# Scores of the first six head pairs: 32-bit matmuls of 64 rows, two side by side, in place of 128 rows half zeros, and a new table of schedule constants

## The chip, the cores and the metric

One core of a Trainium2 chip runs the whole program. The metric is the device time of one execution in microseconds (us); kernels are compared by the median of several executions. One further execution is recorded by the profiler, and all rows below come from it.

## The reference: what is computed

Attention with a threshold, then two feed-forward layers, all in 32-bit floats:

```
q, k, v: (4 batches, 8 heads, 576 positions, 64); tau = 0.02
scores = q @ k^T / sqrt(64)
keep a score if score >= rowmax - tau, else -1e9
attn   = exp(scores - rowmax) / (sum + 1e-9);  x = attn @ v      -> (2304 tokens, 512)
h = x @ w_in   (512 x 2048);  g = relu(h)^2;           x2  = g @ w_out
h = x2 @ w_in2 (512 x 2048);  g = max(0.01 h, h);      out = g @ w_out2
```

## The kernel before

**Attention** is cut into 16 units, one for each batch and pair of heads, and each unit into nine steps: four tiles of 128 query rows of the first head, four of the second, and one step for the last 64 rows of both heads (the tail). That makes 144 steps. In a step the scores of the tile against all 576 keys go into two PSUM banks of 288 columns (tile `s`, L585); VectorE takes the negated row maximum (`nb`, L595), ScalarE the exponential (`e`, L596), VectorE masks it by the threshold `th` and sums it (L602), and small operations give the reciprocal `r` (L605, L608).

For the first six pairs (`nat`, 54 steps) the score matmul runs on plain 32-bit floats. The tile `KH` holds the keys of both heads one above the other, 64 partitions each (head dimension 64), and `Q` holds the queries of a head in its own 64 partitions with zeros in the other 64 (L484). So each matmul contracts over 128 rows, half of them zeros: two matmuls of 128 x 288 for a step (one for each bank), four of 64 x 288 for a tail, where the two heads go to the lower and the upper half of the array's columns. Each 32-bit matmul stands as two records in the trace. From the seventh pair on, scores are products of rounded parts (`KH`, `KL`), and nothing of that is changed.

For the first four pairs (`nav`, 36 steps) the weights `e` are scaled, turned by TensorE (`pt`, L627, L628; five 128 x 128 transposes for a step), copied out (`PT`) and multiplied with the values in 32 bits (`o`, L688: five matmuls with 64 columns, that alternate between the lower and the upper half of the columns, the fifth with 64 rows only). Later pairs split the weights into two 16-bit parts (`P`) that DMA transposes.

**The first feed-forward layer** begins about step 41, in blocks of 256 tokens (`h` L736, `y` L762), on the first 12 of 16 blocks of the hidden dimension, and fills TensorE beside attention. Its weights `w0` to `w11` are unpacked and split on VectorE, ScalarE and GpSimd during the first 60 steps (L372 to L392). After attention the rest of the layer runs in blocks of 512 (L1166, L1208), and the second layer (L1055, L1133).

**The order** is made by a planner when the program is built. Each operation has a priority (its step plus a constant), a cost, and the engines that can do it; `order()` (L118) walks through modelled time, gives each free engine the most urgent ready operation, and weighs engines by the table `price`. The constants in `CFG` (L26) shift priorities, choose which steps split the weights in which way (`lb`), and how many hidden blocks run beside attention (`nf`). The engines then execute in that order, held only by semaphores. A score operation is entered here as two operations of cost 0.486, one for each bank; zeroing `Q` is an operation of its own that VectorE or GpSimd may do. SyncE issues nearly all DMAs; in the first unit the queries of head 0 are issued from ScalarE.

Of the kernel before, what the change touches and what calls it, by code (L numbers as in the profile page):

```python
# [18 lines left out]
P = 128  # L19
# [4 lines left out]
NFA = 12  # L24

CFG = dict(  # L26
    price=[{'V': 3.864, 'A': 2.379, 'G': 2.083},
           {'V': 2.058, 'A': 0.5, 'G': 0.597},
           {'V': 1.454, 'A': 0.877, 'G': 1.005},
           {'V': 4.321, 'A': 0.378, 'G': 0.428},  # L30
           {'V': 1.956, 'A': 0.969, 'G': 2.867},
           {'V': 3.46, 'A': 0.884, 'G': 4.561},
           {'V': 3.025, 'A': 1.381, 'G': 2.849}],
    lead1=0.344, xsg0=[0, 1], lbm=8, lb=[[0, 3, 5, 6], [1, 5], [0, 4], [2, 7]], xsm=4, xsg=[1, 2], dq=0.417, xu=False, pqk=-3.957,
    pd1=1.458, pex=1.266, pd2=1.468, ph=3.893, pl=-2.254, hu=True, bg=6.244, lead=4.309, w0=25.544, wstep=1.408, fend=1.015, tol=-0.227,
    hor=-0.102, xlead=5.334, nb=3, eb=4, pb=3, ptb=3, kvb=3, nat=[0, 1, 2, 3, 4, 5], nav=4, two=False, vb=2, tmb=1, gb=2, xb=1,
    w2step=-3.901, nf=[12, 12, 12, 12], wo=2.009, wold=[9, 10, 16], yal=40.578, xl2=26.294, xp=5, sp=2.609, ws=-16.879, ww=20.813, zc=3.74,
    th=0.397, x2l=2.921, sg0=1.043, sgstep=1.158, zb=1.416, zin=1.434, zout=1.386, slack=0.02, slackd=0.985, wrb=3, r1b=1, xrb=1,
)


# [223 lines left out]
def mmr(n):  # L265
    return (n + 32) / 2400.0


def move(nbytes):
    return nbytes / 220e3  # L270
# [7 lines left out]
def tile_kernel(ctx: ExitStack, tc: tile.TileContext, qT, kT, vv, w1, w2, tau, eye, out):  # L278
    nc = tc.nc
    B, H, D, S = qT.shape  # L280
# [4 lines left out]
    S2 = S // 2  # L285
    MAIN = S // P
    REM = S - MAIN * P
    NH = (S + P - 1) // P
    QB = S + REM
# [4 lines left out]
    f32 = lambda ap: ap.bitcast(F32)  # L294
# [12 lines left out]
    op = plan.op  # L307
# [29 lines left out]
    def dma(o, i, r, w, prio, nbytes, q=nc.sync, **k):  # L337
        return op(("S", 0.06, lambda: q.dma_start(out=o(), in_=i())), r, w, prio, dma=move(nbytes), **k)
# [116 lines left out]
    head, tail = [(0, 0), (0, 1), (1, 0), (1, 1)], [(0, 2), (0, 3), (None, MAIN), (1, 2), (1, 3)]  # L455
# [9 lines left out]
    def prep(n):  # L465
        b, p, what = order[n]
        o = pairs[n] = Box()
        o.b, o.nav, o.own, o.q = b, n < CFG["nav"], n >= NAV, [None] * 2
        h0 = 2 * p
        Q = val("att", "Q2", 2, [P, 2 * S + REM], F32 if n in CFG["nat"] else F32R)  # L470

        o.Q, o.pad = Q, []
        o.qs = qs = lambda h: Q.get()[:, h * QB:h * QB + S]
        at = lambda k: begin[n - 1] - 1.5 + CFG["bg"] + k * len(order[n - 1][2]) / 14 if n else -3.0 + k * 0.1
        raw = lambda: val("stage", "wraw", CFG["wrb"], [P, 2 * S], F32)
        if n in CFG["nat"]:

            kh = val("att", "KH", CFG["kvb"], [P, S], F32R)
            o.KH, o.KL = [kh] * 2, None
            for h in range(2):  # L480

                c0, c1 = (0, S) if len(what) > 5 else (0, 2 * P) if what is head and h == 0 else (REM, REM + 2 * P) if what is head else (2 * P, S) if h == 0 else (0, S)
                z = lambda h=h, c0=c0, c1=c1: qs(h)[(1 - h) * D:(2 - h) * D, c0:c1]
                zero = [("V", 0.55, lambda z=z: nc.vector.memset(z(), 0.0)), ("G", 0.57, lambda z=z: nc.gpsimd.memset(z(), 0.0))]  # L484
                if n:
                    op(zero, [], [Q], at(-1))
                else:
                    zq = Val()
                    o.pad = o.pad + [zq]
                    op(zero[1], [], [zq], at(-1))  # L490
                o.q[h] = c0, c1
            for h in range(2):
                c0, c1 = o.q[h]
                dma(lambda h=h, c0=c0, c1=c1: qs(h)[h * D:(h + 1) * D, c0:c1], lambda h=h, c0=c0, c1=c1: qT[b, h0 + h][:, c0:c1], [], [Q], at(0), D * (c1 - c0) * 4, q=nc.sync if n or h else nc.scalar, urgent=n == 0, issue=0.5 if n or h else 0.06)
            dma(lambda: f32(kh.get()), lambda: kT[b, h0:h0 + 2].rearrange("h d s -> (h d) s"), [], [kh], at(0) if n else -3.1, 2 * D * S * 4, urgent=n == 0)
            op(times(lambda: f32(kh.get()), S)[0:None if n else 1], [kh], [kh], at(1))
        else:
            qr, kr = raw(), raw()
            q3, k3 = (lambda: qr.get().rearrange("p (h s) -> p h s", h=2)), (lambda: kr.get().rearrange("p (h s) -> p h s", h=2))
            for j in range(2):  # L500
                dma(lambda j=j: q3()[j * D:(j + 1) * D], lambda: qT[b, h0:h0 + 2].rearrange("h d s -> d h s"), [], [qr], at(0), 2 * D * S * 4)
            for j in range(2):
                dma(lambda j=j: k3()[j * D:(j + 1) * D], lambda: kT[b, h0:h0 + 2].rearrange("h d s -> d h s"), [], [kr], at(1), 2 * D * S * 4)
            op([("G", 0.145, lambda: nc.gpsimd.memset(f32(Q.get()[:, S:QB]), 0.0))], [], [Q], at(0))
            op(times(kr.get, 2 * S), [kr], [kr], at(2))
            for h in range(2):
                op(rnd(lambda h=h: qs(h), lambda h=h: q3()[:, h], S, engs="AVG"), [qr], [Q], at(2))
            for h in range(2):
                op(sub(lambda h=h: qs(h)[D:P], lambda h=h: q3()[D:P, h], lambda h=h: f32(qs(h)[D:P]), S), [qr, Q], [Q], at(3 + h))
            o.KH, o.KL = [None] * 2, [None] * 2  # L510
            for h in range(2):
                kh = o.KH[h] = val("att", "KH", CFG["kvb"], [P, S], F32R)
                kl = o.KL[h] = val("att", "KL", CFG["kvb"], [P, S], F32R)
                op(rnd(lambda kh=kh: kh.get(), lambda h=h: k3()[:, h], S), [kr], [kh], at(5 + 2 * h))
                op(sub(lambda kl=kl: kl.get(), lambda h=h: k3()[:, h], lambda kh=kh: f32(kh.get()), S), [kr, kh], [kl], at(6 + 2 * h))


        va = o.VA = val("att", "VA", CFG["vb"], [P, NH, 2, D], F32)
        for h in range(2):
            dma(lambda h=h: va.get()[:, 0:MAIN, h], lambda h=h: vv[b, h0 + h, 0:MAIN * P].rearrange("(j p) d -> p j d", p=P), [], [va], at(9), 2 * MAIN * P * D * 4)  # L520
        for rows in (slice(0, REM), slice(P - REM, P)):
            dma(lambda rows=rows: va.get()[rows, MAIN], lambda: vv[b, h0:h0 + 2, MAIN * P:S].rearrange("h p d -> p h d"), [], [va], at(9), 4 * REM * D * 4)
        o.at = at
# [39 lines left out]
    def step(i):  # L563
        n, h, t = steps[i]
        o = pairs[n]
        s = Box()

        ps = val("ps_s", "s", 2, [P, 2, 512], F32)

        g_ = lambda g: slice(g * S2, (g + 1) * S2)  # L570
        if h is not None:
            q0 = h * (QB + REM) + t * P
            lhs = [(h, slice(0, P), slice(q0, q0 + P))]
        elif o.KL:
            lhs = [(0, slice(0, P), slice(MAIN * P, MAIN * P + P)), (1, slice(0, P), slice(S, S + P))]
        else:
            lhs = [(0, slice(0, REM), slice(MAIN * P, S)), (1, slice(REM, P), slice(QB, QB + REM))]

        def qk(g):
            if o.KL:  # L580
                ops = [(r, q, kk[hh]) for hh, r, q in lhs for kk in (o.KH, o.KL)]
            else:
                ops = [(r, q, o.KH[hh]) for hh, r, q in lhs]
            for k, (r, q, kk) in enumerate(ops):
                nc.tensor.matmul(ps.get()[r, g, 0:S2], lhsT=o.Q.get()[:, q], rhs=(kk.get() if o.KL else f32(kk.get()))[:, g_(g)],  # L585
                                 start=k == 0 or not o.KL, stop=k == len(ops) - 1 or not o.KL)
        heads = [hh for hh, _, _ in lhs]
        ks = [o.KH[0]] if o.KL is None else [k for hh in heads for k in (o.KH[hh], o.KL[hh])]
        for g in range(2):
            op(("T", 0.486 if o.KL is None and h is not None else 0.58 if o.KL is None else 2 * len(lhs) * mmr(S2), lambda g=g: qk(g)), [o.Q] + o.pad + ks, [ps], i + CFG["pqk"], True)  # L590
        pv = lambda: ps.get()[:, :, 0:S2]

        nb, th = (val("small", r, 4, [P, 1], F32) for r in ("nb", "th"))
# [4 lines left out]
        k = i % 2  # L598
# [556 lines left out]
    G = {}  # L1155
# [83 lines left out]
    z = [jobs[k * NU + NU - 1][0] + CFG["zb"] + k * CFG["zc"] for k in range(2)]  # L1239
# [20 lines left out]
    for s in range(n2 + 2):  # L1260
        pr = T0 + 2 * s
        work(s)
        if s < n2:
            layer, j, f = items[s]
# [5 lines left out]
        else:  # L1270
            k = s - n2
# [4 lines left out]
    t = n2 + 1.0  # L1276
# [75 lines left out]
```

## Time and profile before

| | |
|---|---|
| median of 3 runs | 1023.25 us (1022.06 to 1023.26) |
| profiled execution | 1027.67 us, of it 1025.9 us from the first to the last instruction |
| TensorE matmul busy | 977.7 us (95%) |
| VectorE | 841.9 us (82%) |
| ScalarE | 707.7 us (69%) |
| GpSimd | 374.9 us (37%) |

Busy time is the time in which an engine had at least one instruction under way; matmuls are pipelined, so a busy TensorE can still do more. The last scores run at 466 us, and from then on TensorE is nearly always busy; it is the 54 steps of the first six pairs, up to some 155 us, that the change is about. The chain of waits is followed back from the last instruction, and a piece on it counts from the end of the piece before.

### The profile page before, as it was taken

The page shows a single profiled execution, that of the slowest core. Times are in us where ns is not written, and L with a number is a line of the kernel's source. Part 1 is how long each engine was busy: PE and PEld are TensorE (multiplying, and loading weights), DVE is VectorE, ACT ScalarE, POOL GpSimd, SP SyncE. Part 2 cuts the span into 40 slices and gives each one's busy share as a digit, 9 for nine tenths or more (in the row PEclk, how much of TensorE's full clock was granted, in tenths as well). Part 3 has the DMA queues.
Part 4 walks back from the last instruction along what each step waited for, and adds up shares of the span by engine and source line. Part 5 has one row for each costly group of instructions (what it writes and reads, how often), then busy time and mean ns, then how long its engine had stood idle before and what let it go on. Part 6 is the DMA issues. An engine that isn't in the chain of part 4 may idle for free.

```text
span 1025.9 us, 20803 instructions
## 1 busy us (share of the span) xinstructions
PE 977.7 (95%) x7436; PEld 848.7 (83%) x7436; DVE 841.9 (82%) x1944; ACT 707.7 (69%) x1379; POOL 374.9 (37%) x476
## 2 busy tenths in 40 slices
PE   7889899889999989999999999999999999999997
PEld 4545578888889978998988888878888888888897
DVE  6988988889999978873675799899979859858756
ACT  5867878877878778884666897867637636536343
POOL 5776888775778679983310000000000000000000
PEclk9999999999999999999999999999999999999999
DMA  6544599988899789756575554430010020010000
GB/s 190 152 147 111 132 211 197 178 158 170 159 167 181 139 175 181 131 102 131 197 250 185 171 184 144 162 126 22 2 63 21 1 84 1 2 63 1 22 23 22
DMA packets 197688, 122.03 MB, mean 119 GB/s; under 512 B 156752, under 2 KB 175312, under 8 KB 197584
## 3 DMA queue, kind: packets, MB, share of 16 engines
q1 hardware_dynamic: 197216, 120.48, 49.2%
q8 instruction: 59, 0.97, 0.4%
q14 instruction: 45, 0.37, 0.1%
q10 hardware_dynamic: 368, 0.21, 0.1%
HBM read 70.98 MB, written 17.83 MB: 87 GB/s over the span
## 4 chain that ended last, share of the span: by engine, by line
PE 66%; DVE 12%; ACT 8%; DMA 5%; issue 5%; POOL 2%; SPq 1%; DVEq 0%; ACTq 0%; POOLq 0%
PE y L1133 9%; PE h L1166 8%; PE y L1208 8%; PE h L1055 7%; PE y L1055 7%; PE h L1133 7%; PE y L762 6%; PE h L736 5%; PE s L585 5%; DVE e L602 3%; DMA PT<-P 3%; DVE nb L595 2%; ACT e L596 2%; DVE P L649 2%; PE o L683 2%
## 5 line engine op out<-in xcount | busy, mean ns | idle before, releaser
L585 PE MATMUL s<-KH,Q 128*128 128x288 f32 (+1 forms) x440 | 125.6, 379 | 23.9 <-DVE e L602 19.5
L596 ACT ACTIVATE e<-s,nb 128x576 f32<-128x576 f32 x144 | 105.6, 738 | 49.2 <-DVE nb L595 31.9
L602 DVE SCALAR_TENSOR_TENSOR e<-s,th,e 128x576 f32<-128x576 f32 x144 | 116.7, 811 | 22.5 <-ACT e L596 16.4
L595 DVE TENSOR_REDUCE nb<-s 128x1 f32<-128x576 f32 x144 | 107.6, 749 | 18.9 <-PE s L585 18.4
L585 PEld LDWEIGHTS s<-KH,Q 128*128 128x128 f32 (+1 forms) x440 | 74.4, 187 | 45.3 <-issue 22.4
L649 DVE SCALAR_TENSOR_TENSOR P<-e,r,P 128x576 f16<-128x576 f32 x81 | 85.7, 1062 | 11.7 <-ACT P L616 10.1
L896 POOL MEMSET yo<- 128x128 f32 x5 | 1.0, 205 | 222.8 <-DVE b L1063 91.3
L683 PE MATMUL o<-PT,V 128*128 128x320 f16 (+1 forms) x432 | 63.3, 292 | 6.4 <-DVE vbound L537 2.9
L1082 ACT ACTIVATE b<-b 128x1024 f32<-128x1024 f32 (+1 forms) x40 | 38.9, 971 | 34.1 <-DVE b L329 33.9
L1133 PEld LDWEIGHTS <-gh 128*128 128x128 f16 x560 | 54.5, 98 | 6.1
L329 DVE TENSOR_TENSOR b<-b 128x256 f32<-128x256 f32 (+1 forms) x120 | 45.3, 389 | 14.9 <-ACT b L1082 14.4
L318 ACT CAST gh<-b 128x512 f16<-128x512 f32 (+1 forms) x77 | 43.5, 564 | 19.1 <-DVE b L329 18.6
L585 PE MATMUL s<-KL,Q 128*128 128x288 f32 x200 | 56.5, 297 | 0.0
L683 PEld LDWEIGHTS <-V 128*128 128x128 f16 x432 | 40.0, 100 | 19.1 <-issue 7.0
L616 ACT ACTIVATE P<-e,r 128x576 f16<-128x576 f32 x55 | 42.4, 773 | 17.3 <-DMA PT<-P 16.3
L329 DVE TENSOR_TENSOR gl<-b,gh 128x384 f16<-128x384 f32 x80 | 48.8, 614 | 0.2 <-ACT gh L318 0.2
L318 ACT CAST xh<-xr 128x512 fp32r<-128x512 f32 (+3 forms) x66 | 37.8, 582 | 15.4 <-DVE xr L329 13.5
L318 ACT CAST gh<-r 128x512 fp32r<-128x512 f32 (+1 forms) x71 | 42.8, 607 | 4.4 <-DVE r L1174 3.6
L331 POOL TENSOR_TENSOR gl<-r,gh 128x512 fp32r<-128x512 f32 x29 | 40.3, 1389 | 10.0 <-ACT gh L318 5.6
L1063 DVE TENSOR_TENSOR b<-h,b 128x256 f32<-128x256 f32 (+1 forms) x96 | 35.3, 372 | 5.5 <-PE h L1055 3.6
L329 DVE TENSOR_TENSOR xl<-xr,xh 128x512 f16<-128x512 f32 (+3 forms) x58 | 37.7, 651 | 1.6 <-ACT xh L318 1.1
L585 PEld LDWEIGHTS s<-KL,Q 128*128 128x128 f32 x200 | 38.4, 192 | 0.0
(1134 smaller groups left out, 3465.6 us busy)
## 6 DMA issues: line engine op xcount, KB each, us to landing
wraw<-w SPq DMA_DIRECT2D x64, 512.0 KB, 4.1
wraw<-qT SPq DMA_DIRECT2D x20, 288.0 KB, 4.1
wraw<-kT SPq DMA_DIRECT2D x20, 288.0 KB, 4.4
out<-yo SPq DMA_DIRECT2D x18, 256.0 KB, 2.3
VA<-vv SPq DMA_DIRECT2D x32, 128.0 KB, 2.8
x2d<-yo SPq DMA_DIRECT2D x16, 256.0 KB, 2.4
xr<-x2d SPq DMA_DIRECT2D x4, 1024.0 KB, 6.2
y1d<-ys SPq DMA_DIRECT2D x14, 256.0 KB, 2.4
```

Of the source, the lines that this page charges most:

```text
L318: alts.append(("A", act(n, psum), lambda: nc.scalar.copy(o(), i()), kind))
L329: alts.append(("V", dve(n), lambda: nc.vector.tensor_tensor(out=o(), in0=a(), in1=b(), op=alu), kind + "*"))
L585: nc.tensor.matmul(ps.get()[r, g, 0:S2], lhsT=o.Q.get()[:, q], rhs=(kk.get() if o.KL else f32(kk.get()))[:, g_(g)], start=k == 0 or not o. ...
L595: op(("V", 0.75, lambda: nc.vector.tensor_reduce(out=nb.get(), in_=pv(), axis=AX.XY, op=ALU.max, negate=True)), [ps], [nb], i + CFG["pd1"] ...
L596: op(("A", 0.74, lambda: nc.scalar.activation(e.get(), pv(), AF.Exp, bias=nb.get(), scale=1.0)), [ps, nb], [e], i + CFG["pex"], True)
L602: op(("V", 0.82, lambda: nc.vector.scalar_tensor_tensor(out=e.get(), in0=pv(), scalar=th.get(), in1=e.get(), op0=ALU.is_ge, op1=ALU.mult, ...
L649: op(("V", 0.8, lambda: nc.vector.scalar_tensor_tensor(out=lo(), in0=ev(), scalar=r_.get()[:, k:k + 1], in1=hi(), op0=ALU.mult, op1=ALU.su ...
L683: nc.tensor.matmul(ps.get()[:, 0:w], lhsT=o.V16.get()[:, k if k < NH else k - NH, h].rearrange("p a d -> p (a d)"), rhs=parts16(pt)[:, k, ...
L1055: nc.tensor.matmul(ps.get()[:, 0:w], lhsT=half(wt)[:, ct + kc * P:ct + (kc + 1) * P], rhs=xt(k)[:, kc], start=fresh and q == 0, stop=q == ...
L1133: nc.tensor.matmul(y.get()[:, c * h:(c + 1) * h], lhsT=l, rhs=r, start=first and c == 0 and q == 0, stop=last and c == len(ks) - 1 and q == 2)
L1166: nc.tensor.matmul(ps.get()[:, 0:n], lhsT=a.get()[:, kc * P:(kc + 1) * P], rhs=x.get()[:, kc, 0:n], start=(q == 0 and kc == 0), stop=(q == ...
L1208: nc.tensor.matmul(o(), lhsT=l, rhs=r, start=(first and q == 0), stop=(last and q == 2))
```

## The change

The keys of a pair are no longer laid one head above the other. Partitions 0 to 63 of `KH` hold the first 288 keys of both heads, partitions 64 to 127 the last 288; `Q` holds both heads in all columns, and the same in both halves of the partitions. A score matmul then contracts over 64 rows: the one for the first bank reads partitions 0 to 63, the one for the second bank partitions 64 to 127, and both together are one operation of the planner (cost 0.69). A tail is four matmuls, one in each quarter of the array. The zeroing of `Q` goes. Keys come in two DMAs in place of one, each with rows of half the length; queries in two DMAs that carry both heads each (in the first unit four), so that twice as many bytes of queries are loaded. The table of constants is new in nearly every entry.

```diff
-    price=[{'V': 3.864, 'A': 2.379, 'G': 2.083},
+    price=[{'V': 4.26, 'A': 2.141, 'G': 1.969},
...
-    w2step=-3.901, nf=[12, 12, 12, 12], wo=2.009, wold=[9, 10, 16], yal=40.578, xl2=26.294, xp=5, sp=2.609, ws=-16.879, ww=20.813, zc=3.74,
+    nf=[12, 12, 12, 10], wo=2.034, wold=[0, 9, 10, 14, 16], yal=40.688, xl2=28.416, xp=5, sp=2.529, ws=-2.249, ww=28.906, zc=3.11, th=0.368,
...
-            for h in range(2):
-                c0, c1 = (0, S) if len(what) > 5 else (0, 2 * P) if what is head and h == 0 else (REM, REM + 2 * P) if what is head else (2 * P, S) if h == 0 else (0, S)
-                z = lambda h=h, c0=c0, c1=c1: qs(h)[(1 - h) * D:(2 - h) * D, c0:c1]
-                zero = [("V", 0.55, lambda z=z: nc.vector.memset(z(), 0.0)), ("G", 0.57, lambda z=z: nc.gpsimd.memset(z(), 0.0))]
-                if n:
-                    op(zero, [], [Q], at(-1))
-                else:
-                    zq = Val()
-                    o.pad = o.pad + [zq]
-                    op(zero[1], [], [zq], at(-1))
-                o.q[h] = c0, c1
-            for h in range(2):
-                c0, c1 = o.q[h]
-                dma(lambda h=h, c0=c0, c1=c1: qs(h)[h * D:(h + 1) * D, c0:c1], lambda h=h, c0=c0, c1=c1: qT[b, h0 + h][:, c0:c1], [], [Q], at(0), D * (c1 - c0) * 4, q=nc.sync if n or h else nc.scalar, urgent=n == 0, issue=0.5 if n or h else 0.06)
-            dma(lambda: f32(kh.get()), lambda: kT[b, h0:h0 + 2].rearrange("h d s -> (h d) s"), [], [kh], at(0) if n else -3.1, 2 * D * S * 4, urgent=n == 0)
+            o.q2 = q2 = lambda: Q.get()[:, 0:2 * S].rearrange("p (h s) -> p h s", h=2)
+            o.k2 = k2 = lambda: f32(kh.get()).rearrange("p (h s) -> p h s", h=2)
+            for g in range(2):
+                rows = slice(g * D, (g + 1) * D)
+                dma(lambda g=g, rows=rows: k2()[rows], lambda g=g: kT[b, h0:h0 + 2, :, g * S2:(g + 1) * S2].rearrange("h d s -> d h s"), [], [kh], at(0) if n else -3.1, D * S * 4, urgent=n == 0)
+            if n:
+                for g in range(2):
+                    rows = slice(g * D, (g + 1) * D)
+                    dma(lambda rows=rows: q2()[rows], lambda: qT[b, h0:h0 + 2].rearrange("h d s -> d h s"), [], [Q], at(0), 2 * D * S * 4, issue=0.5)
+            else:
+                for h in range(2):
+                    for g in range(2):
+                        rows = slice(g * D, (g + 1) * D)
+                        dma(lambda rows=rows, h=h: q2()[rows, h], lambda h=h: qT[b, h0 + h], [], [Q], at(0), D * S * 4, q=nc.sync if h else nc.scalar, urgent=True, issue=0.5 if h else 0.06)
...
+        def tiles():
+            for j in range(2):
+                for g in range(2):
+                    rows = slice(g * D, (g + 1) * D)
+                    if h is None:
+                        a, q, r = j, slice((1 - j) * MAIN * P, (1 - j) * MAIN * P + REM), slice(j * REM, (j + 1) * REM)
+                    elif j == 0:
+                        a, q, r = h, slice(h * REM + t * P, h * REM + (t + 1) * P), slice(0, P)
+                    else:
+                        continue
+                    nc.tensor.matmul(ps.get()[r, g, 0:S2], lhsT=o.q2()[rows, a, q], rhs=o.k2()[rows, a], start=True, stop=True)
+        if o.KL is None:
+            op(("T", 0.69, tiles), [o.Q, o.KH[0]], [ps], i + CFG["pqk"], True)
...
-                nc.tensor.matmul(ps.get()[r, g, 0:S2], lhsT=o.Q.get()[:, q], rhs=(kk.get() if o.KL else f32(kk.get()))[:, g_(g)],
-                                 start=k == 0 or not o.KL, stop=k == len(ops) - 1 or not o.KL)
...
-            op(("T", 0.486 if o.KL is None and h is not None else 0.58 if o.KL is None else 2 * len(lhs) * mmr(S2), lambda g=g: qk(g)), [o.Q] + o.pad + ks, [ps], i + CFG["pqk"], True)
```

What moves in the order of the engines is shown at three places. On TensorE in the first pair, from the tail on, the kernel before has the two halves of a step apart (`s` is the score tile, `pt` the transposes, `o` the values; the numbers behind `Q` only name the buffer):

```order
L585 MATMUL s<-KH,Q_131 64x288 x4
L585 MATMUL s<-KH,Q_131 128x288
L627 MATMUL pt<-eye_sb,e 128x128 x4
L628 MATMUL pt<-eye_sb,e 128x128
L585 MATMUL s<-KH,Q_131 128x288
L627 MATMUL pt<-eye_sb,e 128x128 x4
L628 MATMUL pt<-eye_sb,e 128x128
L688 MATMUL o<-PT,VA 64x256 x5
```

At the same place after the change, where L580 is the new score line and L634, L635 and L695 are the lines called L627, L628 and L688 before:

```order
L580 MATMUL s<-KH,Q_135 64x288 x4
L580 MATMUL s<-KH,Q_135 128x288 x2
L634 MATMUL pt<-eye_sb,e 128x128 x4
L635 MATMUL pt<-eye_sb,e 128x128
L634 MATMUL pt<-eye_sb,e 128x128 x4
L635 MATMUL pt<-eye_sb,e 128x128
L580 MATMUL s<-KH,Q_135 128x288 x2
L695 MATMUL o<-PT,VA 64x256 x5
```

The two halves of a step now always stand together, and the transposes that stood between them come behind.

On TensorE at the start of the fourth pair, some 80 us into the kernel before:

```order
L585 MATMUL s<-KH,Q_672 128x288
L627 MATMUL pt<-eye_sb,e 128x128 x4
L628 MATMUL pt<-eye_sb,e 128x128
L585 MATMUL s<-KH,Q_672 128x288
L688 MATMUL o<-PT,VA 64x256 x5
L627 MATMUL pt<-eye_sb,e 128x128 x4
L628 MATMUL pt<-eye_sb,e 128x128
L585 MATMUL s<-KH,Q_672 128x288 x3
```

And after the change, at the start of the same pair:

```order
L580 MATMUL s<-KH,Q_645 128x288 x2
L634 MATMUL pt<-eye_sb,e 128x128 x4
L635 MATMUL pt<-eye_sb,e 128x128
L634 MATMUL pt<-eye_sb,e 128x128 x4
L635 MATMUL pt<-eye_sb,e 128x128
L580 MATMUL s<-KH,Q_645 128x288 x2
L634 MATMUL pt<-eye_sb,e 128x128 x4
L635 MATMUL pt<-eye_sb,e 128x128
L695 MATMUL o<-PT,VA 64x320 x5
L580 MATMUL s<-KH,Q_645 128x288 x2
```

Between a score step (two groups of 64 rows) and a transpose (128 rows) the array changes its shape at nearly every row; before, only the values `o` and the tails differed in shape from the rest.

On SyncE, which issues the DMAs, the program before begins so (`KH` the keys, `Q` the queries, `wraw` weights of the first layer, `VA` values):

```order
L338 DMA KH<-kT 128x576
L338 DMA Q_131<-qT 64x576
L338 DMA wraw<-w 128x1024 x2
L338 DMA VA<-vv 128x4x64 x2
L338 DMA VA<-vv 64x2x64 x2
L338 DMA KH<-kT 128x576
L338 DMA Q_139<-qT 64x576 x2
```

And after:

```order
L338 DMA KH<-kT 64x2x288 x2
L338 DMA Q_135<-qT 64x576 x2
L338 DMA wraw<-w 128x1024 x2
L338 DMA VA<-vv 128x4x64 x2
L338 DMA VA<-vv 64x2x64 x2
L338 DMA KH<-kT 64x2x288
L338 DMA Q_193<-qT 64x2x576
L338 DMA KH<-kT 64x2x288
L338 DMA Q_193<-qT 64x2x576
```

Two more DMAs stand in front of the first weights, and the DMAs of the second pair carry 288 KB of queries each in place of 144 KB. ScalarE issues two DMAs of queries at the start in place of one.

## Rows read from the trace of the kernel before

**Rows 1.** Windows by stage: busy of PE, PEld, DVE, ACT, POOL; clock, DMA
```profile
core 0: us, PE busy (x) PEld busy (x) DVE busy (x) ACT busy (x) POOL busy (x), PEclk, DMA share, GB/s
5.00:120.00 115.00, 100.18 (x532) 59.43 (x530) 102.36 (x231) 88.05 (x151) 83.06 (x128) 0.99 0.51 147
...
150.00:470.00 320.00, 299.83 (x2341) 280.18 (x2340) 273.27 (x610) 255.29 (x477) 246.40 (x289) 0.99 0.86 163
470.00:1026.00 556.00, 547.18 (x4379) 485.06 (x4376) 439.07 (x1035) 341.05 (x712) 20.57 (x30) 1.00 0.26 84
```

**Rows 2.** Chain of waits, shares by line: 43.6 to 55.5 us, then 71 to 100.5 us
```profile
by line: PE s L585 44.3%; PE o L688 25.4%; PE pt L627 22.7%; issue 6.9%; ACT PT L318 5.9%; PE pt L628 4.6%; DVE nb L595 0.3%
...
by line: PE s L585 43.2%; PE o L688 29.1%; PE pt L627 21.5%; PE pt L628 4.4%; issue 3.5%; DVE e L602 1.8%; DVE nb L595 0.1%
```

**Rows 3.** Windows of the first four pairs, columns as in rows 1
```profile
22.90:43.60 20.70, 17.49 (x93) 10.52 (x93) 19.73 (x41) 17.09 (x31) 13.73 (x24) 1.00 0.55 160
43.60:55.40 11.80, 11.59 (x71) 7.30 (x73) 10.85 (x30) 11.20 (x22) 10.58 (x16) 1.00 0.64 182
55.40:71.00 15.60, 11.55 (x61) 6.59 (x60) 15.46 (x29) 10.78 (x19) 11.32 (x17) 1.00 0.28 75
71.00:100.50 29.50, 29.04 (x159) 17.05 (x161) 24.11 (x60) 21.15 (x36) 20.93 (x32) 0.94 0.45 135
```

**Rows 4.** Windows from the fifth pair on, columns as in rows 1
```profile
100.00:160.00 60.00, 53.56 (x338) 40.79 (x337) 54.11 (x129) 47.70 (x87) 47.66 (x51) 1.00 0.81 177
```

**Rows 5.** Timeline of TensorE, full step: start us, us, instruction
```profile
16.60 0.65 PE L585 MATMUL s<-KH,Q 128*128 128x288 f32 x2
...
16.60 1.14 PE L585 MATMUL s<-KH,Q 128*128 128x288 f32 x4
```

**Rows 6.** Timeline of TensorE, a tail step, columns as before
```profile
19.95 0.46 PE L585 MATMUL s<-KH,Q 128*64 128x288 f32 x2
...
19.95 1.19 PE L585 MATMUL s<-KH,Q 128*64 128x288 f32 x8
```

**Rows 7.** Chain of waits, pieces on TensorE: start us, us, what
```profile
52.12 0.59 PE pt L627 x4
...
53.79 0.46 PE pt L627 x4
...
82.68 0.99 PE s L585 x4
...
90.86 1.91 PE o L688 x10
...
95.77 1.59 PE o L688 x10
```

**Rows 8.** Groups by form in 5 to 150 us: count, busy us, mean ns
```profile
L602 DVE SCALAR_TENSOR_TENSOR e<-s,th,e 128x576 f32<-128x576 f32 x49 | 39.8, 811 | 5.2 <-ACT e L596 4.0 <-POOL th L597 0.6
...
L372 DVE TENSOR_SCALAR wraw<-wraw 128x512 int32<-128x512 int32 x23 | 12.9, 563 | 0.0
...
L484 POOL MEMSET Q<- 64x576 f32 x8 | 4.7, 592 | 0.8 <-POOL t L605 0.5
```

**Rows 9.** Windows at a drop of the clock, columns as in rows 1
```profile
66.90:71.10 4.20, 2.52 (x14) 1.82 (x14) 4.16 (x10) 3.06 (x5) 3.49 (x5) 1.00 0.22 39
71.20:74.60 3.40, 3.40 (x14) 2.07 (x15) 2.30 (x7) 0.27 (x2) 2.52 (x4) 0.51 0.84 294
```

**Rows 10.** The start: timeline of VectorE and TensorE
```profile
4.86 0.52 DVE L450 TENSOR_SCALAR KH<-KH,qsc 128x576 f32<-128x576 f32 x1
...
5.48 0.82 PE L585 MATMUL s<-KH,Q 128*128 128x288 f32 x1
```

**Rows 11.** The start: window, columns as in rows 1
```profile
2.00:5.20 3.20, 3.20 (x9) 1.03 (x7) 0.53 (x3) 1.28 (x1) 1.22 (x3) 1.00 0.89 223
```

**Rows 12.** The start: DMA issues: what, count, KB each, us to landing
```profile
KH<-kT SPq DMA_DIRECT2D x3, 288.0 KB, 3.7
Q<-qT ACTq DMA_DIRECT2D x1, 144.0 KB, 4.0
```

More of the change, by code (lines that the diff above doesn't have):

```diff
@@ L26 @@
 CFG = dict(
-    price=[{'V': 3.864, 'A': 2.379, 'G': 2.083},
[L28 to L36, printed above, removed]
-    w2step=-3.901, nf=[12, 12, 12, 12], wo=2.009, wold=[9, 10, 16], yal=40.578, xl2=26.294, xp=5, sp=2.609, ws=-16.879, ww=20.813, zc=3.74,
-    th=0.397, x2l=2.921, sg0=1.043, sgstep=1.158, zb=1.416, zin=1.434, zout=1.386, slack=0.02, slackd=0.985, wrb=3, r1b=1, xrb=1,
+    price=[{'V': 4.26, 'A': 2.141, 'G': 1.969},
+           {'V': 2.149, 'A': 0.525, 'G': 0.657},
+           {'V': 1.817, 'A': 0.791, 'G': 0.994},
+           {'V': 4.978, 'A': 0.359, 'G': 0.535},
+           {'V': 1.875, 'A': 0.851, 'G': 2.206},
+           {'V': 2.958, 'A': 1.093, 'G': 2.527},
+           {'V': 3.025, 'A': 1.378, 'G': 3.11}],
+    lead1=0.194, xsg0=[0, 1], lbm=8, lb=[[0, 1, 4, 6, 7], [1, 5], [4], [3, 7]], xsm=4, xsg=[1], dq=0.417, xu=True, pqk=-3.957, pd1=2.075,
+    pex=0.67, pd2=1.854, ph=3.829, pl=-2.392, hu=False, bg=5.522, lead=4.309, w0=25.544, wstep=1.281, fend=1.014, tol=0.2, hor=-0.199,
+    xlead=5.334, nb=3, eb=4, pb=3, ptb=3, kvb=3, nat=[0, 1, 2, 3, 4, 5], nav=4, two=False, vb=2, tmb=1, gb=2, xb=1, w2step=-2.074,
+    nf=[12, 12, 12, 10], wo=2.034, wold=[0, 9, 10, 14, 16], yal=40.688, xl2=28.416, xp=5, sp=2.529, ws=-2.249, ww=28.906, zc=3.11, th=0.368,
+    x2l=3.836, sg0=2.669, sgstep=1.117, zb=1.278, zin=0.923, zout=0.928, slack=0.02, slackd=1.05, wrb=3, r1b=1, xrb=1,
 )
@@ L470, in prep @@
         Q = val("att", "Q2", 2, [P, 2 * S + REM], F32 if n in CFG["nat"] else F32R)
-        o.Q, o.pad = Q, []
+        o.Q = Q
         o.qs = qs = lambda h: Q.get()[:, h * QB:h * QB + S]
@@ L570, in step @@
         g_ = lambda g: slice(g * S2, (g + 1) * S2)
[L571 to L575, printed above, removed]
-        else:
-            lhs = [(0, slice(0, REM), slice(MAIN * P, S)), (1, slice(REM, P), slice(QB, QB + REM))]
-        def qk(g):
-            if o.KL:
-                ops = [(r, q, kk[hh]) for hh, r, q in lhs for kk in (o.KH, o.KL)]
-            else:
-                ops = [(r, q, o.KH[hh]) for hh, r, q in lhs]
-            for k, (r, q, kk) in enumerate(ops):
-                nc.tensor.matmul(ps.get()[r, g, 0:S2], lhsT=o.Q.get()[:, q], rhs=(kk.get() if o.KL else f32(kk.get()))[:, g_(g)],
-                                 start=k == 0 or not o.KL, stop=k == len(ops) - 1 or not o.KL)
@@ L587, in step @@
-        heads = [hh for hh, _, _ in lhs]
-        ks = [o.KH[0]] if o.KL is None else [k for hh in heads for k in (o.KH[hh], o.KL[hh])]
-        for g in range(2):
-            op(("T", 0.486 if o.KL is None and h is not None else 0.58 if o.KL is None else 2 * len(lhs) * mmr(S2), lambda g=g: qk(g)), [o.Q] + o.pad + ks, [ps], i + CFG["pqk"], True)
+        def tiles():
[9 more added lines that the diff above has]
+                    nc.tensor.matmul(ps.get()[r, g, 0:S2], lhsT=o.q2()[rows, a, q], rhs=o.k2()[rows, a], start=True, stop=True)
@@ new lines, in step, with qk @@
+        if o.KL is None:
+            op(("T", 0.69, tiles), [o.Q, o.KH[0]], [ps], i + CFG["pqk"], True)
+        else:
+            if h is not None:
+                q0 = h * (QB + REM) + t * P
+                lhs = [(h, slice(0, P), slice(q0, q0 + P))]
+            else:
+                lhs = [(0, slice(0, P), slice(MAIN * P, MAIN * P + P)), (1, slice(0, P), slice(S, S + P))]
+            def qk(g):
+                ops = [(r, q, kk[hh]) for hh, r, q in lhs for kk in (o.KH, o.KL)]
+                for k, (r, q, kk) in enumerate(ops):
+                    nc.tensor.matmul(ps.get()[r, g, 0:S2], lhsT=o.Q.get()[:, q], rhs=kk.get()[:, g_(g)], start=k == 0, stop=k == len(ops) - 1)
+            ks = [k for hh in [hh for hh, _, _ in lhs] for k in (o.KH[hh], o.KL[hh])]
+            for g in range(2):
+                op(("T", 2 * len(lhs) * mmr(S2), lambda g=g: qk(g)), [o.Q] + ks, [ps], i + CFG["pqk"], True)
```

## The prediction

> **What bounds the kernel now.** I read the windows by stage first. From 470 us on TensorE is busy 547 of 556 us and nothing else comes near [rows 1]: whatever the change does there, it does to about 9 us of gaps. From 150 to 470 us TensorE has 300 of 320 us, beside feed-forward work that fills it. The first 120 us are another regime: TensorE 100.2 of 115 us and VectorE 102.4, no filler, and neither full. So the place of the change is the stretch with two nearly equal engines, and the question is how much of a saving on TensorE VectorE lets through.
>
> The second view is the windows of the single stretches of that stage [rows 3]. They alternate. In 71 to 100.5 us TensorE is busy 29.0 of 29.5 us and VectorE 24.1; in 43.6 to 55.4 us TensorE has 11.6 of 11.8, but VectorE 10.9 and ScalarE 11.2 too; in 55.4 to 71 us VectorE has 15.5 of 15.6 us and TensorE only 11.6; in 22.9 to 43.6 us it is VectorE again, 19.7 of 20.7. The chain of waits agrees: in the two TensorE stretches scores make up 44.3% and 43.2% of it [rows 2]. A shorter score pays there and not in the other two.
>
> **The price of a score step.** Two records on the full array show 0.65 us, four show 1.14 [rows 5]: (1.14 - 0.65) / 2 = 0.245 us from one record to the next, so 4 x 0.245 = 0.98 us for a step, and the chain has 0.99 [rows 7]. What two half-arrays do side by side is not shown for halves of the rows, but it is for halves of the columns, in the tails: two records there take 0.46 us together, less than two in sequence, and all eight 1.19 [rows 6]; (1.19 - 0.46) / 3 = 0.243 us for each further pair. So a pair goes in the time of one record. If row halves do the same, a full step takes two units, 0.49 us, and saves 0.49; 48 full steps save 48 x 0.49 = 23.5 us. The bounds of that saving are 0 (the two follow one another) and 0.49. A tail is already four pairs (0.98 us); four quarters at once would make it 0.49, pairs alone leave it: 0 to 2.9 us for six tails, and I take the middle, 1.5, as no row has four at once.
>
> **The price of changing shape.** The values `o` show it: 64 + 64 columns, then a fifth matmul with 64 rows. Chain pieces of 1.91 us (320 wide) and 1.59 us (256 wide) [rows 7] give 0.32 / 64 = 5.0 ns for each column, 1.28 us for 256; 0.31 us are left, and there are two changes of shape in a piece, so 0.155 each. The transposes right behind `o` take 0.59 us and behind scores 0.46 [rows 7], 0.13 more, which agrees. The Trainium skill says why (TensorEngine Tiling (Array Packing), Tiling Modes, Key Properties): a change of the tiling mode drains TensorE. The rows above agree. By that page's table a tiling of 64 rows gives up to twice the speed, which alone would be 25 us here; its drain rule is the part that speaks against this change. Now the count. Over the order of TensorE up to the last of these scores the shape changes 60 times before and 113 times after, since nearly every step now stands between transposes or feed-forward matmuls of 128 rows. So 53 x 0.155 = 8.2 us come back. Bounds: 0, if all changes fall into waits, and 16 at twice the price, since no row shows a 64-row load of 128 columns behind a change.
>
> Net on TensorE: 23.5 + 1.5 - 8.2 = 16.8 us of 54 x 0.98 = 53 us, 32% of each score (from 0 + 0 - 16 at worst to 26.4).
>
> **What of it reaches the end, stage by stage.** VectorE's highest busy share over a window here is 99% (15.46 of 15.60), over the longer ones 95% (19.73 of 20.70) [rows 3]; I let it go to 95%.
> - 71 to 100.5 us: 43.2% of 29.5 us is 12.7 us of scores, of which 32% is 4.1; VectorE's 24.1 us at 95% need 25.4, so 4.1 would just fit. I take 3.5.
> - 43.6 to 55.4 us: 44.3% of 11.8 is 5.2, 32% of it 1.7; ScalarE is at 95% and VectorE at 92% already: 0.4.
> - 22.9 to 43.6 and 55.4 to 71 us: VectorE full, 0. Before 22.9 us the scores at 16.6 and 19.95 us [rows 5, 6] stand on the chain: 2 x 0.31 = 0.6, of which I take 0.5.
> - 100 to 160 us: TensorE 53.6 and VectorE 54.1 of 60 us [rows 4], 16 of the 54 steps, 16 x 0.31 = 5.0 us. Feed-forward work can take the room, but needs VectorE too: 40%, 2.0 us.
> Together 6.4 us.
>
> What VectorE itself does up to step 36 hardly changes: counted over its order, five splits of weights go to GpSimd, and three passes of unpacking and five small operations are added, about as long. Zeroing `Q` ran on GpSimd (eight of twelve in 5 to 150 us, 0.59 us each [rows 8]), not on a bound engine, and its room goes to those splits: nothing.
>
> **The start.** The first score runs at 5.48 us, behind the scaling of the keys at 4.86 [rows 10]. In front of it stood one DMA of keys (288 KB) and one of queries (144 KB) [rows 12]; now 144 KB more of queries of head 0 must come, at the 223 GB/s of 2 to 5.2 us [rows 11] 0.65 us, and nothing else can run. Bounds: 0, where the DMAs of weights step back instead, and 1.3, if the queries of head 1, also doubled, are waited for. I take 0.7. The doubled queries of later pairs are prefetched by some steps, and DMA is at 0.51 of its time in that stage [rows 1]: nothing.
>
> **The rest of the table.** The same 828 `h` and 792 `y` matmuls stand in front of the last score in both orders, so attention carries the same filler; `nf` moves 24 + 24 matmuls of block 6 to the stage where TensorE is full anyway: nothing. Up to step 108 ScalarE's order is 11 operations shorter and VectorE's 6, some 7 us of light work over stages with 20 us of TensorE gaps [rows 1]: I take 1 us gained, bounds -3 and +3, for which no row speaks.
>
> Sum: -6.4 + 0.7 - 1 = -6.7 us. The profiled execution, 1027.7 us with its span of 1025.9, becomes 1021.0. It lies 4.4 us above the median of the runs, 1023.25, and with the same distance the median becomes 1016.6, which I give as 1016.5.
>
> **The rivals.**
> - All of the saving shows: the new order spreads work so that VectorE is never late. For it: VectorE's passes are longer than need be where it meets GpSimd (unpacking L372 has a mean of 563 ns [rows 8]), so its load has slack. Against: 99% and 95% in two stretches. 16.8 + 1 - 0.7 = 17 us: 1006.
> - VectorE is the floor everywhere: each step needs 0.81 us there for the masked pass alone [rows 8], and the maximum and the unpacking come on top. Then only the 2.0 us behind 100 us and the 0.5 at the beginning are left, less the start, 0.7, and the clock may take some: before 71.2 us TensorE was busy 2.5 of 4.2 us, and then the granted clock was 0.51 for 3.4 us, that is 1.2 GHz in place of 2.4 [rows 9]; an emptier TensorE brings more of these, and each costs up to 1.7 us. About 1022.
> - A step takes three units: the second record of the first half has to come before the first of the second half. Saving 0.245 x 48 = 11.8, less 8.2: 3.6 us on TensorE, of which a third, 1.2, shows, less the start: 1022. The Trainium skill (TensorE: Matmul & The Clock Gate, Part 3) says matmuls start and end strictly in program order, which would give this; the column pairs, whose two records take 0.46 us, speak against it here.
> - Slower: row halves don't overlap at all. Nothing is saved, 53 changes cost 8.2 us, all within the chain pieces that end in TensorE; at the share of the forecast (6.4 of 16.8) 3.1 us, in the TensorE stretches themselves up to 8; with the start 4 to 9 us: 1028. It decides from the point where a step takes more than 0.98 - 0.155 = 0.83 us. This is also the case in which the change doesn't do what it says.
>
> **How the numbers follow.** The measurement tells about 0.2%, 2 us, from no change. Forecast 0.64, with its own range 1011 to 1021; whole saving 0.14; VectorE floor 0.09, two thirds of it within 0.2%; three units 0.04, all within; slower 0.09. Faster: 0.61 + 0.14 + 0.03 = 0.78; same 0.03 + 0.06 + 0.04 = 0.13; slower 0.09. The range leaves out most of the slower case and the outer half of the whole saving: 1007 to 1023.
>
> **What would show it.** In the changed profile: pairs of 64-row score records that start together, two in some 0.46 us, four in 0.7; about 0.15 us more for the first transpose behind a score; score records busy 0.5 to 0.65 us a step; TensorE idle more and VectorE above 92% in the first 110 us; the last score at about 460 us in place of 466; the first score at about 6.1 us. The forecast is wrong if score records come one behind another, if VectorE's busy share falls in the first 110 us (then something else waits), or if the stage behind 470 us moves by more than 2 us.

## The result

| | median | runs |
|---|---|---|
| before | 1022.84 us | 6, 1021.43 to 1025.88 |
| changed | 1010.57 us | 6, 1006.05 to 1012.67 |

The ratio is 0.9871 with the interval 0.9842 to 0.9899: 13 us faster, where 6.7 were forecast and 1007 was the lower end. The profiled execution took 1012.67 us with a span of 1010.8; that of before 1027.67 with 1025.9.

The windows by stage of the changed kernel answer to [rows 1] (the last score now runs at 451 us, so the last two stages are cut at 460):

```profile
5.00:120.00 115.00, 92.64 (x541) 48.17 (x540) 102.30 (x247) 88.93 (x152) 89.30 (x122) 0.91 0.65 177
...
150.00:460.00 310.00, 298.93 (x2378) 281.82 (x2377) 266.14 (x601) 253.27 (x467) 240.78 (x285) 1.00 0.87 166
460.00:1011.00 551.00, 540.55 (x4318) 477.95 (x4317) 437.12 (x1032) 336.13 (x700) 22.50 (x30) 1.00 0.26 83
```

TensorE has 7.5 us less in the first 115 us, at a clock of 0.91; VectorE has as much as before there. From 150 us to about the last score TensorE's gaps fall from 20 us of 320 to 11 of 310.

Counted by steps of attention (start of the exponential, L596 before and L603 after), the changed kernel is 0.4 us late at the first step, 1.1 us early at step 45, 6.1 at step 54, 11.1 at step 81 and 17.2 at the last; the stages behind give 2 back. So in these two executions little of the gain stands where most of the changed matmuls do. Each trace is of one execution, and the changed one was the slowest of its six. The stage from step 45 to the last, before and after, one window of each trace (columns as in rows 1):

```profile
136.90:469.80 332.90, 312.42 (x2427) 291.21 (x2425) 285.34 (x642) 266.93 (x498) 256.83 (x300) 0.99 0.87 164
```

```profile
135.80:452.50 316.70, 304.69 (x2415) 284.84 (x2414) 275.74 (x629) 260.72 (x478) 249.45 (x296) 1.00 0.88 168
```

It is 16.2 us shorter: TensorE's busy time by 7.7 and its gaps by 8.5, from 20.5 to 12.0 us. The longest wait there is the same in both, TensorE's score matmul for VectorE to free a score tile, shorter by half in the changed kernel. From 135 to 460 us, total, times and longest in us, before and after (after the change the first six pairs have a line of their own, L580):

```profile
PE s L585 <- DVE e L602: 12.1, 16, 2.3
```

```profile
PE s L594 <- DVE e L609: 5.3, 13, 0.8
...
PE s L580 <- DVE e L609: 0.6, 1, 0.6
```

**The matmuls themselves** do what the forecast took. The timeline of TensorE in the changed kernel, for a full step and a tail; of each first the records that start together, then all (start us, us, instruction):

```profile
25.44 0.51 PE L580 MATMUL s<-KH,Q 64*128 64x288 f32 x2
...
25.44 0.76 PE L580 MATMUL s<-KH,Q 64*128 64x288 f32 x4
...
21.67 0.47 PE L580 MATMUL s<-KH,Q 64*64 64x288 f32 x4
...
21.67 0.72 PE L580 MATMUL s<-KH,Q 64*64 64x288 f32 x8
```

Two records of different halves end within 0.51 us, and the other two 0.25 us later, where the full array needed 1.14 us for four [rows 5]. A tail's quarters run four at a time: eight records in 0.72 us, 1.19 before [rows 6]. The price of changing shape is on the chain:

```profile
21.74 0.69 PE s L580 x8
...
25.40 0.11 PE pt L635
25.51 0.69 PE s L580 x4
26.19 1.59 PE o L695 x10
27.78 0.59 PE pt L634 x4
28.37 0.11 PE pt L635
28.48 1.19 PE s L580 x8
...
29.77 0.63 PE pt L634 x4
```

A lone step has 0.69 us there, 0.49 of work and 0.20 behind the change; two steps together have 1.19, so the second costs the bare 0.5. The values `o`, which already changed shape before, cost the same 1.59 as in [rows 7]. So a lone step went from 0.97 to 0.69 us on the chain, and the transposes behind a step from 0.46 [rows 7] to 0.63.

**The clock** is the other visible difference. The first window of the changed kernel:

```profile
5.00:22.90 17.90, 13.64 (x63) 6.75 (x61) 13.11 (x30) 9.32 (x15) 9.54 (x17) 0.71 0.88 211
```

The granted clock has a mean of 0.71 here; before it was 1.00, with 14.1 us of TensorE busy. In the trace the clock is at half, 1.2 GHz, for 10.2 us from 9.7 us on, and for 13.6 more up to 125 us; before, once, for 3.4 [rows 9]. Between steps 45 and 143 it is the other way round: the changed kernel's clock is never at half there, that of before twice, which is up to 3.4 us of the 16.2 by which that stage differs:

```profile
187.30:190.70 3.40, 3.40 (x14) 2.91 (x15) 2.59 (x7) 1.43 (x3) 1.65 (x3) 0.50 0.93 206
245.30:248.70 3.40, 3.10 (x13) 2.14 (x13) 3.18 (x12) 2.07 (x3) 1.95 (x4) 0.50 1.25 208
```

### The profile page after: what moved, and what is told of

The parts are those of the page before. It is cut to its first block, busy times and chain, and to the rows that moved or that the text cites. A ratio compares the mean times of both kernels' runs of the same rounds, so it can differ in the third digit from the quotient of the medians.

```text
span 1010.8 us, 20761 instructions
## 1 busy us (share of the span) xinstructions
PE 963.6 (95%) x7436; PEld 831.2 (82%) x7436; DVE 834.7 (83%) x1948; ACT 704.1 (70%) x1361; POOL 377.4 (37%) x467
## 4 chain that ended last, share of the span: by engine, by line
PE 61%; DVE 17%; ACT 9%; issue 5%; DMA 5%; POOL 2%; SPq 0%; DVEq 0%; ACTq 0%; POOLq 0%
PE y L1140 8%; PE y L1062 7%; PE h L1140 7%; PE h L1062 7%; PE h L743 6%; PE h L1173 6%; PE y L1215 6%; PE y L769 5%; DVE e L609 3%; DVE P L656 3%; DMA PT<-P 3%; DVE nb L602 3%; PE s L594 2%; PE o L690 2%; ACT e L603 2%
## 5 line engine op out<-in xcount | busy, mean ns | idle before, releaser
L603 ACT ACTIVATE e<-s,nb 128x576 f32<-128x576 f32 x144 | 106.0, 740 | 27.1 <-DVE nb L602 17.9
L594 PE MATMUL s<-KH,Q 128*128 128x288 f32 x200 | 59.2, 314 | 6.2 <-DVE e L609 5.3
L318 ACT CAST gh<-b 128x384 f16<-128x384 f32 (+1 forms) x78 | 44.0, 564 | 19.1 <-DVE b L329 18.5
L580 PE MATMUL s<-KH,Q 64*128 64x288 f32 (+1 forms) x240 | 43.0, 483 | 12.3 <-DVE e L609 5.2
L318 ACT CAST xh<-xr 128x512 f16<-128x512 f32 (+3 forms) x65 | 36.9, 580 | 16.5 <-DVE xr L329 14.7
L594 PEld LDWEIGHTS s<-KH,Q 128*128 128x128 f32 x200 | 37.7, 189 | 10.8 <-DVE e L609 4.2
L329 DVE TENSOR_TENSOR gl<-r,gh 128x512 fp32r<-128x512 f32 (+1 forms) x44 | 31.4, 715 | 14.9 <-ACT gh L318 14.7
L604 POOL TENSOR_SCALAR th<-nb,ca 128x1 f32<-128x1 f32 x70 | 32.5, 466 | 24.4 <-DVE nb L602 16.6
```

The lines of the kernel that those rows point to most:

```text
L318: alts.append(("A", act(n, psum), lambda: nc.scalar.copy(o(), i()), kind))
L329: alts.append(("V", dve(n), lambda: nc.vector.tensor_tensor(out=o(), in0=a(), in1=b(), op=alu), kind + "*"))
L603: op(("A", 0.74, lambda: nc.scalar.activation(e.get(), pv(), AF.Exp, bias=nb.get(), scale=1.0)), [ps, nb], [e], i + CFG["pex"], True)
```

## The experiments

Each ratio is to the kernel before, run beside it on the same chip. "Idle" is span less busy time of TensorE between steps 45 and 143, worked out from a window of the run's trace as for the two kernels above. The ratio is from all runs of a kernel, the last three columns are from one execution each, so differences of some us in them can be that execution's own.

| run | ratio, interval | first 45 steps, us | steps 45 to 143, us | idle, us |
|---|---|---|---|---|
| before | 1 | 128.9 | 332.9 | 20.5 |
| changed | 0.9871 (0.9842 to 0.9899) | 127.4 | 316.7 | 12.0 |
| e1 new scores, old table | 1.004 (1.0023 to 1.0056) | 123.0 | 340.0 | 26.0 |
| e2 old scores, new table | 0.999 (0.9978 to 1.0002) | 122.0 | 331.6 | 17.9 |
| e3 nf 12 | 0.9909 (0.9889 to 0.9929) | 127.3 | 314.9 | 10.4 |
| e4 new, small shift | 0.9982 (0.9966 to 0.9998) | 126.6 | 326.0 | 20.8 |
| e5 old, small shift | 1.005 (1.0029 to 1.0071) | 127.1 | 333.1 | 21.7 |
| e6 old, latency 0.025 | 1.0004 (0.9988 to 1.0021) | 127.3 | 330.8 | 20.6 |
| e7 new, latency 0.025 | 0.9949 (0.9933 to 0.9965) | 124.1 | 325.7 | 17.0 |
| e8 new, first 36 twice | 0.9955 (0.9934 to 0.9976) | 132.6 | 317.2 | 12.1 |
| e9 old, latency 0.030 | 1.0066 (1.0035 to 1.0097) | 126.2 | 340.0 | 22.1 |
| e10 new, latency 0.030 | 0.9996 (0.9975 to 1.0017) | 123.8 | 331.8 | 21.2 |
| e11 new, latency 0.015 | 0.9919 (0.9894 to 0.9944) | 125.8 | 323.3 | 16.7 |
| e12 new, first 4 twice | 0.9879 (0.9853 to 0.9904) | 125.1 | 318.5 | 12.9 |
| e13 new, all 54 twice | 0.9971 (0.9955 to 0.9986) | 132.4 | 316.7 | 8.5 |
| e14 new, old choices | 0.9918 (0.9899 to 0.9938) | 123.0 | 320.7 | 17.0 |

**e1, e2: the two halves of the change alone.** e1 is the changed code with the whole `CFG` of before, e2 the code before with the whole new `CFG`.

> The new score matmuls with the constants of the kernel before, all of them. Theory A (my forecast was right for the matmuls, and the other 6 us are the table's): about 1017 us, ratio to before 0.993 to 0.996, first 54 steps some 5 us shorter, 150 to 460 us as before. Theory B (the matmuls give it all, because steps that end earlier also free later stages): about 1011 us, ratio 0.988. Theory C (the old constants do not fit the new costs): 1023 us or more, ratio 1.00 or above.

> The scores of the kernel before (128 rows, half zeros) with the new constants. Theory A: some 6 us faster than before, 1016 to 1018 us, and the gain lies behind 150 us. Theory B: no faster than before, 1021 to 1025 us. Theory C (the constants only fit the new costs): slower than before, 1026 us or more.

Neither half gives anything alone: e1 came out as theory C had it, e2 as theory B. Theory A falls: the parts do not add up. With the old constants the new matmuls cost 4 us (e1), with the new ones they gain 12 (changed against e2). But e1 is not slow everywhere. Its first 45 steps are 5.9 us shorter, and then steps 45 to 143 take 7 us longer than before, with 26 us idle. The short first steps do not speak for the matmuls alone: those of e2, with the old matmuls, are 6.9 us shorter. Steps 45 to 143 of e1:

```profile
131.50:471.50 340.00, 314.01 (x2454) 291.66 (x2452) 286.71 (x648) 268.52 (x501) 264.49 (x292) 0.99 0.85 162
```

The constants fix an order by modelled time; with another cost of a score every later decision falls differently. So the question became how much any order is worth.

**e3: `nf` back to 12.**

```diff
-    nf=[12, 12, 12, 10]
+    nf=[12, 12, 12, 12]
```

> The changed kernel with 12 in place of 10 hidden blocks beside attention in the last block of 256 tokens (nf), all else as changed. If moving these 24 + 24 matmuls is worth nothing, as the prediction had it: the time of the changed kernel, ratio to before 0.985 to 0.990. If the stage right behind attention was the one that gained (the last h of that stage is 23 us earlier in the changed trace, the last score 17): some 3 us slower, ratio about 0.991.

1013.3 us and 0.9909, as the second case had it: 3.9 us slower than the changed kernel by the ratios. But the intervals overlap and the profiled executions are level (spans of 1010.6 and 1010.8 us), so whether the moved matmuls are worth anything is not settled.

**e4 to e7, e9 to e11: neighbours.** Three small shifts, each on the old and on the new kernel (and a fourth on the new alone), give other orders at the same costs:

```diff
-    pqk=-3.957
+    pqk=-3.9
```

```diff
-    slack=0.02
+    slack=0.025
```

(0.03 in e9 and e10, 0.015 in e11.)

> The changed kernel with one constant moved a little (priority of the scores, -3.957 to -3.9 steps), which gives another order on every engine from the first pair on, at the same costs. It measures how much of a table's time is the luck of one order. If a table's gain is a matter of balance (which engine does what): within 3 us of the changed kernel, ratio 0.985 to 0.991. If it is that one order: most of the table's 6 us are gone, ratio 0.992 or above.

> The kernel before with the same small shift as e4 (priority of the scores -3.957 to -3.9), so another order at the same costs. If the old table, like the new one, is one well-placed order (theory D: each table was picked among many orders, and any neighbour is some 8 to 11 us worse): 1029 to 1034 us, ratio above 1.006. If the old order is nothing special (theory E: the new table is a lucky draw, and the matmuls themselves are worth little): 1020 to 1026 us, ratio 0.997 to 1.003.

> The kernel before with another small shift: the latency that the planner adds in front of TensorE, 0.020 to 0.025 us. Theory D: 1029 to 1034 us. Theory E: 1020 to 1026 us.

> The changed kernel with the same shift as e6 (0.020 to 0.025 us). Theory D: about 1021 us like e4, 6 to 10 us below e6, which is then what the matmuls are worth between two orders that nobody picked. Theory E: anywhere between 1012 and 1026 us, and not clearly below e6.

> The kernel before with the planner's latency in front of TensorE at 0.030 in place of 0.020 us. If the matmuls are worth 6 to 8 us between orders that nobody picked (theory D as e5 to e7 have left it: neighbours of the old order lie 0 to 4 us above it): 1022 to 1028 us. If the old scores can fall to 1017 or less with some neighbour, the spread of orders is too wide to speak of a worth.

> The changed kernel with the same shift as e9 (0.030 us). Theory D: 1015 to 1021 us, 5 to 10 us below e9, with 17 to 21 us of idle TensorE between steps 45 and 143 in place of 12. If the new table is good in general and e4, e7 were bad luck: 1009 to 1013 us.

> The changed kernel with that latency at 0.015 us: TensorE's order is the changed kernel's up to the first feed-forward matmuls and differs only from there, so the first 45 steps should take what they take there (127 us). Theory D (the last 6 us of the gain sit in how feed-forward work is placed between steps 45 and 143): 1015 to 1021 us, and all of the difference in that stage. If not: 1009 to 1013 us.

All four neighbours of the changed kernel are slower than it, by 5 to 13 us; those of the old one by 0.4 to 7. Taken by pairs with the same shift, new to old: e4 to e5 0.993, e7 to e6 0.995, e10 to e9 0.993, on average 0.9936, or 6.6 us. That is close to the forecast of 6.7, between orders that nobody picked, but it is the average of three pairs that differ in their tables too, and each ratio is uncertain by about 0.2 to 0.3%. The output of e5 is off by 12%, why is open, so its pair tells of the time alone; without it the average is 0.9938, or 6.4 us. The parts of theory D that ask for 8 to 11 us around the old table do not hold, since e6 is level with it, and e9 and e10 both ended some 3 us above the range expected of them. Where the neighbours lose is shown best by e11, whose order on TensorE differs only from the first feed-forward matmuls on: 125.8 us for the first 45 steps, no worse than the changed kernel, then 6.6 us more, 4.7 of them idle (its clock is at half for 6.8 us of that stage, so the rest can be the clock). The same stage in e4, with 20.8 us idle:

```profile
135.10:461.10 326.00, 305.22 (x2403) 283.42 (x2402) 280.60 (x625) 257.55 (x477) 252.74 (x298) 1.00 0.84 163
```

**e8, e13: the order kept, the saving taken away.** The score matmuls are issued twice into the same tile, in the first 36 steps (e8, the edit shown) and in all 54 (e13, with `[0, 1] * 2`). All else on the engines stays in the changed kernel's order, in the traces too:

```diff
-            for j in range(2):
+            for j in [0, 1] * (2 if i < 36 else 1):
```

> The changed kernel, in the same order, with the score matmuls of the first 36 steps issued twice into the same tile (the second result replaces the first): 0.49 us more of TensorE a step, 17 us in all, with no further change of shape. If the shorter TensorE is what made the first 100 us shorter (my forecast's stages, 4 us): 4 to 8 us slower, about 1016. If VectorE is the floor of the first 100 us, so that the saving there showed nowhere: within 2 us of the changed kernel; and if the emptier TensorE lost time by its clock (24 us at half clock in the first 125 us of the changed trace), fewer such drops and the same time or up to 3 us faster.

> The changed kernel, same order, the score matmuls of all 54 steps issued twice (26 us more of TensorE, about what the change had taken off it before the changes of shape). It leaves the order and takes the saving away. If order and saving add up: e8 lost 7 us for 36 steps; the other 18 stand beside feed-forward work, where TensorE is the fuller engine, and cost up to 0.49 each: 1018 to 1027 us, the stage from step 54 on unchanged. If the order is only good together with the saving, the stage from step 54 on loses its 6 us as well: 1028 us or more.

These decide. In e13 TensorE has its old score work again and the changes of shape on top, 26.4 us more than the changed kernel (0.49 us in each of 54 steps), and the time is 1.0% longer (0.9971 to 0.9871), about 10 us: 39% of what was added, 26 to 51% with both intervals. The forecast had 6.4 of 16.8 us, 38%. In e8 it is 8.6 of 17.6 us, 49%; the last 18 steps add only 1.6 of their 8.8, which is not clear of noise. The granted clock is also higher with the added work (mean 0.992 to 0.997 over the runs of e13, 0.987 to 0.993 over those of the changed kernel), so these prices are net of that. By the forecast's sum e13 has 9.6 us more on TensorE than the kernel before (26.4 less 16.8), and it is still 3 us faster than that kernel (0.9971, interval 0.9955 to 0.9986): this much the order, with what else is new, gives at the least. And the stage from step 45 on is 316.7 us, to the tenth that of the changed kernel, and as long as in e8 within 0.5:

```profile
142.20:458.90 316.70, 308.22 (x2456) 288.47 (x2455) 278.21 (x629) 259.88 (x479) 246.89 (x296) 1.00 0.89 168
```

So the gain in that stage does not stand on the saved matmul time: it goes with the order, but for the up to 3.4 us that the clock cost the kernel before there. And VectorE is not the only floor of the first 100 us either: 36 steps with 17.6 us more on TensorE made the first 45 steps 5 us longer.

**e12: the clock.** As e8, with `i < 4`.

> The changed kernel, same order, the score matmuls of the first four steps issued twice (2 us more of TensorE while it has nothing else to do). If the 10.2 us of half clock from 9.7 us on come from the emptier TensorE in front of them, they are gone, and the ninth step, 1.6 us behind the kernel before in the changed trace, is level with it or ahead: 1 to 3 us faster than the changed kernel, ratio 0.984 to 0.987. If the drop stays: 1 us slower, ratio 0.988 to 0.990.

The drop at 9.7 us is gone, in the same order, with more work on TensorE:

```profile
5.00:22.90 17.90, 12.37 (x83) 7.33 (x82) 14.86 (x34) 10.85 (x17) 10.87 (x19) 1.00 0.85 210
```

Step 9 (the first is step 0) comes 1.4 us earlier than in the changed kernel, step 81 2.0 us; at step 117 nothing of it is left (120.9 us between the two, 118.6 in the changed kernel), and the time is the same; the 1 to 3 us expected did not come. From 5 us to the drop at 9.7 TensorE was busy 1.95 us in the changed kernel, and 2.34 us from 5 to 9.7 us in e12. So the emptier TensorE as the cause of this drop is supported, but not shown: e11, with the same matmuls in the same order on TensorE there and none of them twice, was busy 3.04 us in that window and has no drop either, and its step 9 is only 0.3 us earlier than the changed kernel's. The price of the drop at the end of the program is not above the spread of the runs.

**e14: which constants.** `lb`, `xsg`, `xu` and `hu` as before.

> The changed kernel with the old values of the four constants that choose how and where the weights are split and the outputs joined (lb, xsg, xu, hu), all other constants new. If these choices made the late stage better (fewer operations on ScalarE and GpSimd): 18 to 22 us of idle TensorE between steps 45 and 143 and 1017 to 1023 us, as for the other neighbours. If the rest of the table did it: still 12 us idle and 1009 to 1013 us.

17.0 us idle and a median of 1014.4, between the cases. The idle time is that of e7 and e11, which have the new choices, so e14 does not tell whether these choices or only another order costs it. Its first 45 steps are in the changed kernel's order on TensorE and take 4.4 us less, with 10.2 us at half clock in the first 125 where the changed kernel's profile has 23.8. The changed kernel's own runs are spread by 6.6 us, from 1006.05 us at a mean clock of 0.993 to 1012.67 at 0.988; that the clock makes this spread is likely, not shown.

## Why the prediction was wrong

- *The price of a score step.* Right: two units, 0.49 us. The tails save nearly the full 2.9 us (0.47 in each of six), where the middle, 1.5, was taken.
- *The price of changing shape.* Right in kind and size: 0.20 us in front of a lone step and about 0.15 behind, 0.155 each was taken. With the tails' 1.3 us more and some 1 us more for the changes, the 16.8 us net on TensorE stands; this is a sum, no window shows it alone.
- *What of it reaches the end.* 6.4 us were forecast. Between neighbours with the same shift it is 6.6 us; in the fixed order 39% of what is put back, which for 16.8 us is 6.5 (4 to 9 with the intervals). So the size agrees with what was measured, within a wide margin; with one and the same table it came out anywhere from 4 us lost to 12 gained. That the two averages meet the forecast so closely is partly luck. The places were right only in part. Before 71 us the changed kernel's TensorE ran at half clock for 13.6 us, and in 71 to 100.5 us, where 3.5 us were expected, the clock was full but VectorE the fuller engine, so the profiled changed kernel is only 2.4 us early at step 36. Neighbours with the same scores are up to 6.1 us early there, but so is e2, with the old scores, by 6.0.
- *The start.* The first score came 1.25 us later (6.73 us), the upper bound of 1.3; 0.7 was taken, for more bytes of queries. By the chain it waited for the keys, whose DMA took 4.47 us there and whose scaling came at 6.16 us in place of 4.86. The first exponential came only 0.4 us later, since the score itself was shorter.
- *VectorE as the floor*, at 95% busy. Right in a stretch, wrong for the stage: it stayed at 89% in the first 115 us, before and after, but where TensorE was the fuller engine before, in 71 to 100.5 us [rows 3], VectorE now is:

```profile
71.00:100.50 29.50, 23.94 (x153) 12.73 (x154) 28.36 (x69) 22.87 (x38) 25.49 (x35) 1.00 0.61 176
```

- *The rest of the table.* **This is the step that failed.** It had "1 us gained, bounds -3 and +3, for which no row speaks". The whole change gives 13 us; less 6.5 for the matmuls, the order gives some 6.6, an estimate as uncertain as that 6.5; e13 shows 3 of it without any split. The last score runs at 451 us, where about 460 was named. I argued from counts of operations, which hardly change; what changed was which operation stands before which in the stage behind, and TensorE's gaps there, 12 us in place of 17 to 26 in all other orders tried except e3, e8, e12 and e13, which keep this one (8.5 to 12.9). The bounds were taken too narrow: neighbours of one table differ by 8 us (e10, e11), and the changed kernel's table lies at the lower end of its own neighbours.
- *The rivals.* The rows of the changed kernel rule out three units for a step and halves that do not overlap. The Trainium skill (TensorE: Matmul & The Clock Gate, Part 3) says that matmuls start and end strictly in program order; the prediction made three units of it by placing both records of the first half before those of the second. Here two records of different halves end within 0.51 us, so they don't stand that way; the trace does not contradict the page, as the records of a step end in the order in which they start. That the changed kernel would see more drops of the clock was right, 24 us at half clock in place of 3.4 in the first 125.

What stays open is why this order has fewer gaps. All waits of TensorE for VectorE from 135 to 460 us are shorter by 6.8 us in it (10.8 in place of 17.6), but no single constant was found that makes it, and e14 does not decide on the four that it sets back.

## What to carry to other kernels

When a change comes with a new table for a planner, two prices have to be forecast: the work, from rows, and the order, from the spread among neighbours of a table (here 0.6% among three of the old table, 0.8% among four of the new), at whose good end this table lay. To measure the first alone, keep the order and put the work back (issue it twice), or compare both kernels under the same small shifts, with enough pairs: three left it uncertain by some us here. Packing two halves of the array pays two units in place of four, less the change of shape on either side, so put packed steps next to each other.

## What was not expected of the hardware

- The four quarters of the array run 32-bit matmuls all at once: eight records of 288 columns in 0.72 us.
- More work on TensorE need not make a stretch longer: with 2 us of doubled matmuls at the start the granted clock up to 22.9 us was 1.00 in place of 0.71, and step 9 came 1.4 us earlier, in one execution of each.
- Runs of one program differ by 0.7% (1006.05 to 1012.67 us in six runs of the changed kernel, 0.8% in the 29 of the old one beside e1 to e4). The changed kernel's two fastest runs have its two highest mean clocks, 0.993 and 0.991; the old one's runs differ as much at 0.995 to 1.000.
